# Second layer of three token blocks by seven half-size products instead of one full product

## The chip, the cores and the metric

The kernel runs on one core of one Trainium2 chip. The metric is the device time of one execution, in microseconds (us). The engines of the core are named as in the profile: PE (TensorE, matrix products), PEld (its weight loads), DVE (VectorE), ACT (ScalarE), POOL (GpSimd) and SP (SyncE, whose queue issues most transfers).

## The reference

Attention in two scales over 8 batches, 8 heads, 576 positions of 64 columns, then a two-layer network with ELU over all 4608 tokens:

```python
# attention, per head: a coarse one over means of 4 positions, repeated 4 times,
# and a local one over positions with |i - j| < 4
out_up = np.repeat(sm_attn(q_d, k_d, v_d), 4, axis=2)
x = (out_up + out_local)            # -> [4608 tokens, 512]
h = x @ w_in                        # [4608, 2048]
g = np.where(h > 0.0, h, np.exp(np.minimum(h, 0.0)) - 1.0)
return g @ w_out                    # [4608, 512] float32
```

## The kernel before, in words

The tokens are cut into nine blocks (0 to 8) of 512 tokens; a head batch `b` gives 576 tokens, so blocks and head batches overlap in time. Three kinds of work share the engines.

*Attention* (head batches 0 to 7): loads, casts from float32 to float16 on POOL (`cast_qk` L241, `cast_v` L302), transposes and scores on PE, exponentials on ACT, a mask on DVE (L496), denominators, outputs on PE into two-bank PSUM tiles, and `normalise` (L663): DVE multiplies by the reciprocals (L666, L671) and POOL adds local and coarse part into the block's input `xt` (L683).

*First layer*, `mm1(t, fc)` (L704): for block `t` and each of 16 groups `fc` of 128 hidden columns, four matmuls of 128x128 weights by 512 tokens (L719) fill a PSUM bank `hp` (two such banks, in turn). ELU follows in three operations: ACT takes the exponential (L723), DVE clamps it and subtracts one (L724), DVE takes max(h, 0) plus that (L725) into `gts[t][:, fc, :]`, in float16, hidden columns on the partitions.

*Second layer*, `mm2(t, i)` (L729): for each of four groups of 128 tokens, 16 matmuls (L739), four in each step `i`, take 128x128 of `gts[t]` as weights and 512 columns of `WO` (w_out) as the moving operand and add into a bank `op`; ACT copies it to `os` (L745) and SP sends it out (L747). The last token group of block 8 is done in two column parts, 384 and 128.

The order of everything is written by hand. Each piece of work is an event with a number, `at(number, function, ...)`; the events are sorted by number (L1014) and each engine runs its instructions in the order in which they were traced, so a waiting instruction holds all those behind it on its engine. The numbers are a plan, about one unit for each step of the first layer: `mm1_at(t, i)` is `51.52 + 16*(t-3) + i` for blocks from 4 on, and `mm2_at(t, i)` is `mm1_at(t+1, 0) + 0.5 + i`. So step `i` of the first layer of block `t+1` alternates on PE with step `i` of the second layer of block `t`. Below, "slot" is such a unit counted from the first layer step 0 of the block in hand. The second layer of block 8 has no first layer beside it and is the tail. The attention of a head batch is placed by a list of numbers (`LATER`, L977, for batches 4 to 6, `LAST`, L978, for batch 7), relative to the first layer of the block of the same number; `cast`, `tr`, `sc` and `out` are the casts, transposes, scores and outputs of its four head pairs.

Memory is taken from pools of tiles; a tile with the same tag and `bufs=n` takes turns in n places and waits until the place is free. PSUM has eight banks: two `misc`, two tiles of two banks for attention (`two`, L134), and from the end of batch 0 on two `hp` banks.

## Time and profile before

| | us |
|---|---|
| timed runs, median of three | 354.37 |
| timed runs, lowest and highest | 353.4 and 357.04 |
| profiled execution, span from the first to the last instruction | 353.6 |
| first layer of block 6 begins (PE, L719) | 249.15 |
| first layer of block 7 begins | 281.46 |
| last copy from PSUM begins (ACT, L745) | 350.81 |

The profile gives no time outside the span. In its rows "L739" is line 739 of the kernel, "out<-in" are the tiles written and read, and a busy time with "x4" is that of four instructions merged into one row. "idle before" is time in which the engine stood still ahead of the instruction, with the instruction that ended it behind the arrow. Matmuls overlap in the pipeline of PE, so a matmul's own duration is longer than its distance to the next; the distance is what counts.

### The profile page before, as it was taken

The numbers are of one execution on the slowest core, as the hardware profiler recorded it, in microseconds if no ns is written. First come the engines' busy times: TensorE is split into PE (matmuls) and PEld (weight loads), VectorE is DVE, ScalarE is ACT, GpSimd is POOL, SyncE is SP. The second block draws the span as 40 slices with busy tenths as digits, with TensorE's granted clock in tenths as the row PEclk, the third lists the DMA queues.
The fourth block names the chain that finished last, engine by engine and source line by source line (L and its number), as shares of the span: only waits on it lengthen the run. The fifth ranks groups of instructions, "written<-read, shape, count | busy, mean of one in ns | idle before, by whom it ended". The sixth has DMA issues, their size and how long they took to land.

```text
span 353.6 us, 10486 instructions
## 1 busy us (share of the span) xinstructions
PE 335.8 (95%) x4288; PEld 185.3 (52%) x4288; DVE 236.2 (67%) x466; ACT 180.6 (51%) x312; POOL 160.0 (45%) x298
## 2 busy tenths in 40 slices
PE   8897998899889998899999999999999999999996
PEld 4665784455455544445555555545455544444443
DVE  2316999665878775977797789779756955555510
ACT  3572795256665653466355636663553444444421
POOL 4563458286875841973396449755300600000000
PEclk9998999879989999999999999999999999999999
DMA  9999997899998869898979797953014010010012
GB/s 177 201 209 192 213 208 152 200 213 190 188 185 158 167 139 181 168 190 158 196 150 214 158 214 155 168 131 54 30 35 116 32 59 31 32 52 37 32 59 89
DMA packets 98768, 48.89 MB, mean 138 GB/s; under 512 B 81617, under 2 KB 93217, under 8 KB 98721
## 3 DMA queue, kind: packets, MB, share of 16 engines
q1 hardware_dynamic: 94417, 41.86, 58.7%
q0 software_dynamic: 4064, 6.26, 10.0%
q8 instruction: 33, 0.54, 0.7%
q10 hardware_dynamic: 240, 0.11, 0.2%
q14 instruction: 14, 0.11, 0.1%
HBM read 41.97 MB, written 9.55 MB: 146 GB/s over the span
## 4 chain that ended last, share of the span: by engine, by line
PE 75%; DVE 13%; DMA 6%; issue 3%; ACT 3%; SPq 0%; DVEq 0%; ACTq 0%
PE op L739 31%; PE hp L719 28%; DVE gt L725 4%; DMA rcb<-rd 3%; DVE e L724 3%; DVE ln L671 2%; DMA rd<-rc 2%; PE sc L758 2%; PE tqk L328 2%; PE sc L458 2%; PE lg L602 1%; ACT e L723 1%; PE vs L405 1%; PE lg L622 1%; PE den L518 1%
## 5 line engine op out<-in xcount | busy, mean ns | idle before, releaser
L739 PE MATMUL op<-WO,gt 128*128 128x512 f16 (+2 forms) x592 | 146.0, 375 | 0.5 <-DVE gt L725 0.5
L723 ACT ACTIVATE e<-hp 128x512 f16<-128x512 f32 x144 | 86.2, 599 | 107.1 <-PE hp L719 95.3
L719 PE MATMUL hp<-xt,WI 128*128 128x512 f16 x512 | 133.7, 385 | 1.4 <-DVE gt L725 1.3
L725 DVE SCALAR_TENSOR_TENSOR gt<-hp,e 128x512 f16<-128x512 f32 x144 | 99.6, 692 | 6.4
L724 DVE TENSOR_SCALAR e<-e 128x512 f16<-128x512 f16 x144 | 60.6, 421 | 58.4 <-ACT e L723 58.0
L739 PEld LDWEIGHTS <-gt 128*128 128x128 f16 x592 | 55.4, 98 | 61.7 <-issue 1.6
L719 PEld LDWEIGHTS <-WI 128*128 128x128 f16 x512 | 55.6, 115 | 50.0 <-issue 3.2
L683 POOL TENSOR_TENSOR xt<-ln 128x128 f16<-128x128 f16 (+7 forms) x55 | 36.6, 693 | 56.9 <-DVE ln L671 56.9
L481 ACT ACTIVATE pex<-sc 128x580 f16<-128x580 f32 (+1 forms) x56 | 30.1, 594 | 9.2 <-PE sc L471 8.6
L302 POOL CAST v<-v 128x640 f16<-128x640 f32 (+1 forms) x32 | 23.7, 741 | 20.4 <-DMA v<-in_v_dram 13.6
L394 POOL TENSOR_TENSOR t<-qt 128x288 f32<-128x288 f16 x27 | 18.1, 670 | 31.4 <-ACT qt L358 31.4
L745 ACT COPY os<-op 128x512 f32<-128x512 f32 (+2 forms) x37 | 21.4, 578 | 18.9 <-PE op L739 18.8
L377 DVE TENSOR_REDUCE ke<-kt 128x145 f16<-128x580 f16 x28 | 21.0, 751 | 2.4 <-ACT kt L365 2.4
L358 ACT COPY qt<-tqk 128x576 f16<-128x576 f16 x28 | 17.9, 639 | 8.4 <-PE tqk L328 7.7
L671 DVE TENSOR_TENSOR ln<-lg,rcb 128x580 f16<-128x580 f32 x28 | 21.1, 752 | 0.0
L241 POOL CAST k<-k 96x768 f16<-96x768 f32 x24 | 19.8, 825 | 0.1
L241 POOL CAST q<-q 96x768 f16<-96x768 f32 x24 | 19.6, 818 | 0.0
L698 PE MATMUL hp<-xt,WI 128*128 128x256 f16 x128 | 17.0, 283 | 0.7 <-DVE v L276 0.4
L496 DVE TENSOR_TENSOR pex<-pex,MASK 128x580 f16<-128x580 f16 x28 | 13.6, 486 | 3.0 <-ACT pex L481 2.8
L698 PEld LDWEIGHTS <-WI 128*128 128x128 f16 x128 | 13.3, 116 | 1.9 <-issue 0.8
L396 POOL TENSOR_TENSOR qd<-t 128x144 f16<-128x144 f32 x27 | 12.1, 448 | 2.1
L458 PEld LDWEIGHTS <-kt 64*64 64x64 f16 x560 | 6.9, 109 | 11.2 <-issue 8.6
(113 smaller groups left out, 273.4 us busy)
## 6 DMA issues: line engine op xcount, KB each, us to landing
out_dram<-os SPq DMA_DIRECT2D x35, 256.0 KB, 2.1
v<-in_v_dram SPq DMA_DIRECT2D x111, 80.0 KB, 4.5
q<-in_q_dram SPq DMA_DIRECT2D x25, 288.0 KB, 3.9
k<-in_k_dram SPq DMA_DIRECT2D x25, 288.0 KB, 5.0
rcb<-rd SPq DMA_DIRECT2D x10, 364.0 KB, 5.1
WI<-in_moe_w_in_dram POOLq DMA_DIRECT2D x4, 512.0 KB, 7.9
WO<-in_moe_w_out_dram POOLq DMA_DIRECT2D x4, 512.0 KB, 7.4
q<-in_q_dram POOLq DMA_DIRECT2D x7, 144.0 KB, 8.5
```

Of the source, the lines that this page charges most:

```text
L241: nc.gpsimd.tensor_copy(out=x[:], in_=src)
L302: nc.gpsimd.tensor_copy(out=v16[:], in_=v32[:].rearrange("p (e c) d -> p c e d", e=2))
L481: nc.scalar.activation(out=s["p"][:, :, a : a + n], in_=g2(sc, a, n), func=AF.Exp, scale=SCALE / 16 if a else SCALE,)
L671: nc.vector.tensor_tensor(out=ln[:, 0 : 2 * WL].rearrange("p (m h u) -> p m h u", h=2, u=WQ), in0=_free(lg[:, 0:1], [[WQ, WM], [512, 2], [ ...
L683: eng.tensor_tensor(out=xt(t)[:, j, t0 - TBLK * t : t1 - TBLK * t], in0=ln[:, a:z], in1=_rep4(ln[:, ga : ga + (z - a) // 4]), op=AB.add,)
L698: nc.tensor.matmul(FS[i][:, 256 * f : 256 * f + 256], w_in(dc, 2 * n + f), xts[0][:, dc, 256 * h : 256 * h + 256], start=(f == dc == 0), s ...
L719: nc.tensor.matmul(hp, w_in(dc, fc), xts[t][:, dc, :], start=(dc == 0), stop=(dc == DMC - 1),)
L723: nc.scalar.activation(out=e, in_=hp, func=AF.Exp)
L724: nc.vector.tensor_scalar(out=e, in0=e, scalar1=1.0, scalar2=-1.0, op0=AB.min, op1=AB.add)
L725: nc.vector.scalar_tensor_tensor(out=to, in0=hp, scalar=0.0, op0=AB.max, in1=e, op1=AB.add)
L739: nc.tensor.matmul(op_[:, a:z], gts[t][:, fc, 128 * tt : 128 * tt + 128], WO[:, fc, a:z], start=(fc == 0), stop=(fc == FCN - 1),)
L745: nc.scalar.copy(out=os_[:, a:z], in_=op_[:, a:z])
```

## The change

The second layer of blocks 6, 7 and 8 (`SW = 6`) is computed as a product of 2x2 halves. Tokens, hidden columns and output columns are halved (256, 1024, 256), and seven products of sums and differences of the halves (Winograd's form of Strassen's scheme) take the place of eight. A block has two units `u` of 128 rows of each token half. A product of a unit is eight matmuls of 128x128 weights by 256 columns: 112 matmuls of 256 columns a block instead of 64 of 512.

- `weights_7`: eight DVE subtractions of 128x1024 float16 make four difference matrices of `WO`, once. They stand from 0.6 to 14.6 units after the last cast of batch 7, that is from slot 11.75 of block 5's first layer to slot 9.75 of block 6's, two units apart.
- `sums_7`: for each group of four first-layer steps, four operations of 128x512 float16 make the sums of `gts[t]`; one of them overwrites a quarter of it. Groups 0 to 2 run on POOL, group 3 on DVE.
- the first layer of blocks 6 to 8 takes the hidden groups in the order 0, 8, 1, 9, ..., so that partners come together.
- `product` and `finish`: products 1, 6, 5, 3 add up in one half of a bank `y`, product 2 and products 7, 4 in the two halves of a bank `xz`; ACT copies the state after 1, 6 and 7 to SBUF; DVE adds in `finish` 4 (128x512) and `finish` 5 (128x256), ACT copies in `finish` 3. For blocks 6 and 7 the products of a unit stand at slots 0.5, 1.5, 2.5, 3.5, 4.5, 5.5 and 7.5 (plus 8 for the second unit), in the order 1, 2, 7, 6, 4, 5, 3; `finish` 4 and 5 stand 0.6 behind their product, `finish` 3 stands 0.1 behind. For block 8 both units are interleaved in the tail.
- `y` and a second tile `hx` take the four banks that attention used, once it is over; blocks 7 and 8 use `hx` as two further banks of the first layer.
- in blocks 7 and 8, for steps with `i % 8` in (1, 2, 5, 6, 7), ELU runs as Relu(-h) and Exp(-that) on ACT and one DVE operation, max(e - 1, h).
- tiles that are dead by then move to pools (`lo`, `tu`) which are closed, and the new tiles lie in their place.

The diff, cut to its core:

```diff
+SW = 6
+BELOW = (1, 2, 5, 6, 7)
...
-    def mm1(t, fc):
+    def mm1(t, i):
+        fc = i if t < SW else i // 2 + 8 * (i % 2)
...
-            hp, to = bank("hp", "hp")[:], gts[t][:, fc, :]
+            spare = late.get("x") if i % 4 > 1 else None
+            hp = spare[:, 512 * (i % 2) :][:, 0:512] if spare else bank("hp", "hp")[:]
+            to = gts[t][:, fc, :]
...
+        if t > SW and i % 8 in BELOW:
+            r = sb.tile([128, TBLK], FP32, tag="os", bufs=3, name="r")[:]
+            nc.scalar.activation(out=r, in_=hp, func=AF.Relu, scale=-1.0)
+            nc.scalar.activation(out=e, in_=r, func=AF.Exp, scale=-1.0)
+            nc.vector.scalar_tensor_tensor(
+                out=to, in0=e, scalar=-1.0, op0=AB.add, in1=hp, op1=AB.max
+            )
+            return
...
+    def weights_7(n, c):
+        T, k = W7["T"], slice(4 * c, 4 * c + 4)
+        b11, b12 = WO[:, k, 0:MH], WO[:, k, MH:DM]
+        b21, b22 = WO[:, FH + 4 * c :, 0:MH][:, 0:4], WO[:, FH + 4 * c :, MH:DM][:, 0:4]
+        x, y = ((b12, b11), (b22, T[:, 0, k]), (b22, b12), (b21, T[:, 1, k]))[n]
+        nc.vector.tensor_tensor(out=T[:, n, k], in0=x, in1=y, op=AB.subtract)
+
+    def sums_7(t, g):
...
+        S, G, k, l = S7[t], gts[t], slice(2 * g, 2 * g + 2), slice(FH + 2 * g, FH + 2 * g + 2)
+        a11, a12, a21, a22 = G[:, k, 0:TH], G[:, l, 0:TH], G[:, k, TH:TBLK], G[:, l, TH:TBLK]
+        eng = nc.vector if g == 3 else nc.gpsimd
+        for to, x, y, op in (
+            (S[:, 0, k], a21, a22, AB.add), (a21, a11, a21, AB.subtract),
+            (S[:, 1, k], S[:, 0, k], a11, AB.subtract), (S[:, 2, k], a12, S[:, 1, k], AB.subtract),
+        ):
+            eng.tensor_tensor(out=to, in0=x, in1=y, op=op)
+
+    def close_attention():
+        late["x"], late["y"] = two("hx"), two("y")
...
+    def product(t, u, n, k0=0, k1=FH):
+        xz, y, sn, ou = unit(t, u)
+        G, S, T = gts[t], S7.get(t), W7["T"]
+        a, b = slice(128 * u, 128 * u + 128), slice(TH + 128 * u, TH + 128 * u + 128)
+        to = y[:, 0:MH] if n in (1, 3, 5, 6) else xz[:, 0:MH] if n == 2 else xz[:, MH:DM]
+        for k in range(k0, k1):
+            w, x = (
+                (G[:, k, a], WO[:, k, 0:MH]), (G[:, FH + k, a], WO[:, FH + k, 0:MH]),
+                (S[:, 2, k, a], WO[:, FH + k, MH:DM]), (G[:, FH + k, b], T[:, 3, k]),
+                (S[:, 0, k, a], T[:, 0, k]), (S[:, 1, k, a], T[:, 1, k]), (G[:, k, b], T[:, 2, k]),
+            )[n - 1]
+            nc.tensor.matmul(
+                to, w, x, start=(k == 0 and n in (1, 2)), stop=(k == FH - 1),
+                skip_group_check=n > 2,
+            )
+        if k1 == FH and n in (1, 6, 7):
+            nc.scalar.copy(out=sn[:, {1: 0, 6: 1, 7: 2}[n], :], in_=to)
+
+    def finish(t, u, n):
...
+        if n == 4:
+            nc.vector.tensor_tensor(
+                out=ou[:, :, 0:MH], in0=xz[:].rearrange("p (c m) -> p c m", c=2), in1=sn[:, 0:2, :],
+                op=AB.add,
+            )
+        if n == 5:
+            nc.vector.tensor_tensor(out=ou[:, 1, MH:DM], in0=to, in1=sn[:, 2, :], op=AB.add)
+            nc.sync.dma_start(out=out[z : z + 128], in_=ou[:, 1, :])
+            if (t, u) == (NT - 1, 1):
+                nc.sync.dma_start(out=out[r : r + 128, 0:MH], in_=ou[:, 0, 0:MH])
+        if n == 3:
+            nc.scalar.copy(out=ou[:, 0, MH:DM], in_=to)
+            m0 = MH if (t, u) == (NT - 1, 1) else 0
+            nc.sync.dma_start(out=out[r : r + 128, m0:DM], in_=ou[:, 0, m0:DM])
...
-            if 16 * t + i <= 16 * NT - 4:
+            if t < SW:
                 at(mm2_at(t, i), mm2, t, i)
+    at(PLAN[B - 1]["cast"][3] + 0.05, close_feed)
+    at(PLAN[B - 1]["tr"][3] + 0.05, close_turn)
+    for n in range(4):
+        for c in range(2):
+            at(PLAN[B - 1]["cast"][3] + 0.6 + 2 * (2 * n + c), weights_7, n, c)
+    for t in range(SW, NT):
+        for g in range(4):
+            x = mm1_at(t, 4 * g + 3) + 0.05
+            if (t, g) == (SW, 2):
+                x = max(x, max(PLAN[B - 1]["out"]) + 0.1)
+            at(x, sums_7, t, g)
+        z = mm2_at(t, 0)
+        if t < NT - 1:
+            for u in range(2):
+                for n, x in zip((1, 2, 7, 6, 4, 5, 3), (0, 1, 2, 3, 4, 5, 7)):
+                    at(z + 8 * u + x, product, t, u, n)
+                    if n in (4, 5, 3):
+                        at(z + 8 * u + x + (0.1 if n == 3 else 0.6), finish, t, u, n)
+        else:
+            steps = [(u, n, 0, FH - 1) for u in range(2) for n in (1, 2)]
+            steps += [(u, n, FH - 1, FH) for u in range(2) for n in (1, 2)]
+            steps += [(u, n) for u, n in ((0, 7), (0, 6), (1, 7), (1, 6), (0, 4), (0, 5), (1, 4), (1, 5), (0, 3), (1, 3))]
+            for n, x in enumerate(steps):
+                at(z + n, product, t, *x)
+                if x[1] in (4, 5, 3):
+                    at(z + n + 0.1, finish, t, *x)
+    at(mm1_at(SW + 1, 0) - 0.1, close_attention)
```

More of the change, by code (lines that the diff above doesn't have):

```diff
@@ L120, in const @@
     def const(a, name, queue):
-        t = C[name] = sb.tile(list(a.shape), FP16, tag=name, bufs=1, name=name)
+        pool = sb if name in ("ID", "MASK", "IND2", "VR2") else lo
+        t = C[name] = pool.tile(list(a.shape), FP16, tag=name, bufs=1, name=name)
         queue.dma_start(out=t[:], in_=nc.inline_tensor(a, name=name + "c").ap())
+    feed = ctx.enter_context(ExitStack())
+    turn = ctx.enter_context(ExitStack())
+    lo = feed.enter_context(tc.tile_pool(name="lo", bufs=1, side="right"))
+    tu = turn.enter_context(tc.tile_pool(name="tu", bufs=1))
     front = ctx.enter_context(ExitStack())
@@ L175, in load_wo @@
         nc.gpsimd.dma_start(out=WO[:, 4 * n : 4 * n + 4, :], in_=src)
-    KD = [sb.tile([128, 2 * KG + 16], FP16, tag=f"kd{i}", bufs=1, name="kd") for i in range(4)]
+    KD = [lo.tile([128, 2 * KG + 16], FP16, tag=f"kd{i}", bufs=1, name="kd") for i in range(4)]
     KE = [sb.tile([128, 192], FP16, tag=f"ke{i}", bufs=1, name="ke") for i in range(4)]
@@ L391, in sums @@
         else:
-            t2 = sb.tile([128, 2 * SD], FP32, tag="pex", bufs=2, name="t2")
+            t2 = tu.tile([128, 2 * SD], FP32, tag="pex", bufs=2, name="t2")
             at_ = src.rearrange("p (g f) -> p f g", f=2)
@@ L730, in mm2 @@
         tt, part = i // 4, i % 4
-        cols = ((0, DM),)
-        if t == NT - 1 and tt == 3:
-            cols, part = ((0, 384), (384, DM)), 0
-        for a, z in cols:
-            if part == 0:
-                ops[(t, tt)] = bank("misc", "op")
-            op_ = ops[(t, tt)]
-            for fc in range(4 * part, 4 * part + 4 if len(cols) == 1 else FCN):
-                nc.tensor.matmul(
-                    op_[:, a:z], gts[t][:, fc, 128 * tt : 128 * tt + 128], WO[:, fc, a:z],
-                    start=(fc == 0), stop=(fc == FCN - 1),
-                )
-            if part == 3 or len(cols) == 2:
-                os_ = sb.tile([128, DM], FP32, tag="os", bufs=3, name="os")
-                nc.scalar.copy(out=os_[:, a:z], in_=op_[:, a:z])
-                r = TBLK * t + 128 * tt
-                nc.sync.dma_start(out=out[r : r + 128, a:z], in_=os_[:, a:z])
+        if part == 0:
+            ops[(t, tt)] = bank("misc", "op")
@@ new lines, in mm2 @@
+        op_ = ops[(t, tt)]
+        for fc in range(4 * part, 4 * part + 4):
+            nc.tensor.matmul(
+                op_[:], gts[t][:, fc, 128 * tt : 128 * tt + 128], WO[:, fc, :],
+                start=(fc == 0), stop=(fc == FCN - 1),
+            )
+        if part == 3:
+            os_ = sb.tile([128, DM], FP32, tag="os", bufs=3, name="os")
+            nc.scalar.copy(out=os_[:], in_=op_[:])
+            r = TBLK * t + 128 * tt
+            nc.sync.dma_start(out=out[r : r + 128], in_=os_[:])
@@ new lines, with close_feed, close_turn @@
+    W7, S7, U7 = {}, {}, {}
+    MH, TH, FH = DM // 2, TBLK // 2, FCN // 2
+    def close_feed():
+        feed.close()
+        late["w"] = ctx.enter_context(tc.tile_pool(name="w7", bufs=1, side="right"))
+        W7["T"] = late["w"].tile([128, 4, FH, MH], FP16, tag="T", name="w7")
+    def close_turn():
+        turn.close()
+        late["s"] = ctx.enter_context(tc.tile_pool(name="s7", bufs=1))
+    def weights_7(n, c):
[4 more added lines that the diff above has]
+        nc.vector.tensor_tensor(out=T[:, n, k], in0=x, in1=y, op=AB.subtract)
@@ new lines, in sums_7 @@
+    def sums_7(t, g):
+        if g == 0:
+            S7[t] = late["s"].tile([128, 3, FH, TH], FP16, tag="S", bufs=2, name="s7")
+        S, G, k, l = S7[t], gts[t], slice(2 * g, 2 * g + 2), slice(FH + 2 * g, FH + 2 * g + 2)
[6 more added lines that the diff above has]
+            eng.tensor_tensor(out=to, in0=x, in1=y, op=op)
@@ new lines, in close_attention, with unit @@
+    def close_attention():
+        late["x"], late["y"] = two("hx"), two("y")
+    def unit(t, u):
+        if (t, u) not in U7:
+            z, y = bank("misc", "xz"), late["y"][:, 512 * u :][:, 0:512]
+            sn = late["s"].tile([128, 3, MH], FP32, tag="sn", bufs=2, name="sn")
+            ou = late["s"].tile([128, 2, DM], FP32, tag="ou", bufs=2, name="ou")
+            U7[(t, u)] = z, y, sn, ou
+        return U7[(t, u)]
+    def product(t, u, n, k0=0, k1=FH):
[9 more added lines that the diff above has]
+            )[n - 1]
+            nc.tensor.matmul(
+                to, w, x, start=(k == 0 and n in (1, 2)), stop=(k == FH - 1),
[3 more added lines that the diff above has]
+            nc.scalar.copy(out=sn[:, {1: 0, 6: 1, 7: 2}[n], :], in_=to)
@@ L750 @@
     act, dve = nc.scalar.copy, nc.vector.tensor_copy
-    Z = sb.tile([128, 512], FP16, tag="Z", bufs=1, name="Z")
+    Z = lo.tile([128, 512], FP16, tag="Z", bufs=1, name="Z")
     def keep(t, n):
@@ L826, in selections @@
         else:
-            src = sb.tile([KW, 16], FP16, tag="I4", bufs=1, name="I4")
+            src = lo.tile([KW, 16], FP16, tag="I4", bufs=1, name="I4")
             nc.vector.tensor_reduce(
```

24 lines of the change are left out of this document (14 added, 10 removed).

## The prediction

> **What bounds the kernel now.** I read the busy shares first, then the chain that ended last, then a table of busy time over the stretches of the last blocks.
>
> ```profile
> span 353.6 us, 10486 instructions
> PE 335.8 (95%) x4288; PEld 185.3 (52%) x4288; DVE 236.2 (67%) x466; ACT 180.6 (51%) x312; POOL 160.0 (45%) x298
> ...
> PE 75%; DVE 13%; DMA 6%; issue 3%; ACT 3%; SPq 0%; DVEq 0%; ACTq 0%
> ```
> ```profile
> 213.00:247.40 34.40, 34.35 (x472) 17.92 (x471) 28.32 (x51) 19.59 (x35) 24.28 (x47) 1.00 0.68 130
> 247.40:280.70 33.30, 33.27 (x395) 17.14 (x395) 23.77 (x47) 15.48 (x27) 7.11 (x13) 1.00 0.19 56
> 280.70:308.40 27.70, 27.70 (x130) 13.49 (x128) 16.36 (x33) 11.91 (x20) 0.96 (x1) 1.00 0.10 39
> 308.40:336.00 27.60, 27.60 (x129) 13.46 (x128) 15.78 (x32) 11.91 (x20) 0.00 (x0) 1.00 0.10 39
> 336.00:354.00 18.00, 14.73 (x85) 7.45 (x82) 0.99 (x2) 3.69 (x7) 0.00 (x0) 1.00 0.19 73
> ```
> In the second fence the columns behind the stretch are its length and the busy time of PE, PEld, DVE, ACT and POOL, then the granted clock. In the first layer of blocks 6, 7 and 8 (stretches two, three and four) and in the tail TensorE never waits, at full clock. Any time it is given less work is won, and any wait that it gets is lost, one for one. DVE is the next engine: 28.3 of 34.4 us in the stretch with the outputs of head batch 6, 16 of 28 later.
>
> **Part 1, fewer columns through TensorE: minus 4.4 us.** One regular slot, and the only products of 256 columns with a full 128x128 weight tile, at full clock:
>
> ```profile
> 331.54 1.03 PE L719 MATMUL hp<-xt,WI 128*128 128x512 f16 x4
> 331.83 0.69 DVE L725 SCALAR_TENSOR_TENSOR gt<-hp,e 128x512 f16<-128x512 f32 x1
> ...
> 332.40 1.03 PE L739 MATMUL op<-WO,gt 128*128 128x512 f16 x4
> 332.60 0.60 ACT L723 ACTIVATE e<-hp 128x512 f16<-128x512 f32 x1 [1.13 <-PE hp L719]
> ...
> 333.23 0.29 DVE L724 TENSOR_SCALAR e<-e 128x512 f16<-128x512 f16 x1 [0.70 <-ACT e L723]
> 333.26 1.03 PE L719 MATMUL hp<-xt,WI 128*128 128x512 f16 x4
> 333.56 0.69 DVE L725 SCALAR_TENSOR_TENSOR gt<-hp,e 128x512 f16<-128x512 f32 x1
> ```
> ```profile
> 37.21 3.68 PE L698 MATMUL hp<-xt,WI 128*128 128x256 f16 x32 [0.31 <-DVE gt L725]
> 41.28 1.03 PE L698 MATMUL hp<-xt,WI 128*128 128x256 f16 x8 [0.39 <-DVE v L276]
> ```
> ```profile
> L698 PEld LDWEIGHTS <-WI 128*128 128x128 f16 x128 | 13.3, 116 | 1.9 <-issue 0.8
> ```
> From 331.54 to 333.26 are eight matmuls of 512 columns: 1.72 us, 0.216 each (the last one's shown end includes its drain). Of 256 columns, 24 more take 3.68 - 1.03 = 2.65 us, 0.110 each, so weight loads don't bind. A block's second layer goes from 64 x 0.216 = 13.8 us to 112 x 0.110 = 12.4: 1.45 saved, 4.4 in three blocks. Bounds: 5.2 if 256 columns cost just half (0.108), 2.5 if each costs the 0.116 that its weight load shows.
>
> **Part 2, a new wait in each unit: plus 6.8 us.** A unit's y bank takes product 1, then 6, 5 and 3 on top; between 5 and 3 DVE must have read it (finish 5). By the order of events, product 5 stands at slot 5.5, finish 5 at 5.5 + 0.6 = 6.1, the first layer's step 6 at 6.0, product 3 at 7.5. So finish 5 is queued on DVE behind the ELU of step 6, whose matmul runs only after product 5; and step 6 is one of those (i mod 8 in 1, 2, 5, 6, 7) with two ACT passes. Product 3 waits for all of it, with everything behind it on PE's queue.
>
> ```profile
> L745 ACT COPY os<-op 128x512 f32<-128x512 f32 x35 | 20.6, 590 | 16.5 <-PE op L739 16.4
> L671 DVE TENSOR_TENSOR ln<-lg,rcb 128x580 f16<-128x580 f32 x28 | 21.1, 752 | 0.0
> L666 DVE TENSOR_TENSOR ln<-lg,rcb 128x144 f16<-128x144 f32 x28 | 8.4, 300 | 6.2 <-DMA rcb<-rd 3.9 <-PE lg L622 2.2
> L791 ACT CAST vd<-vs 96x256 f16<-96x256 f32 x4 | 1.5, 364 | 0.0
> L238 ACT ACT_TABLE_LOAD x1 | 1.3, 1283 | 1.6 <-PEq L1030 1.6
> ```
> ```profile
> 250.22 0.60 ACT L723 ACTIVATE e<-hp 128x512 f16<-128x512 f32 x1 [0.23 <-PE hp L719]
> 250.71 1.07 ACT L481 ACTIVATE pex<-sc 128x580 f16<-128x580 f32 x2
> ```
> ```profile
> 242.06 0.75 DVE L671 TENSOR_TENSOR ln<-lg,rcb 128x580 f16<-128x580 f32 x1
> 242.73 0.76 DVE L724 TENSOR_SCALAR e<-e 128x512 f16<-128x512 f16 x1
> ```
> From the end of step 6 on PE (the slot above: 332.40): ACT starts after 0.20; Relu 0.60 (as the copy of that shape, L745); Exp, now from SBUF, 0.63 (the trace has none of this shape; from below 0.5, if it begins in its forerunner's last 0.1 as the ACT rows at 250 do, from above 0.7); 0.03 to DVE; the last ELU operation 0.69; finish 5, 128x256 from PSUM, 0.42 (0.300 + 112 x 452/436 ns, between L666 and L671), beginning 0.08 before its forerunner's end as the second of the two DVE rows does; about 0.08 to PE. Sum 2.57. PE has step 7 to do meanwhile, 0.86. Wait 1.7 us a unit, four units (two each for blocks 6 and 7, in the steps of blocks 7 and 8): 6.8 us. Bounds: 4 x 1.4 = 5.6 and 4 x 2.2 = 8.8 (another ACT or DVE instruction of 0.5 in front). What product 3 holds up is all later PE work, so nothing gives it back. The other edges are covered: product 6 needs ACT's copy of product 1, three slots (5 us) earlier, 0.36 (L791); finish 4 (0.69) frees no bank of this unit.
>
> The Trainium skill, "ScalarE: Activation LUTs", section "Rules for kernel authors", says to do relu on VectorE and not ScalarE, which speaks against moving the clamp. By the profile's rows VectorE takes 0.29 where Relu takes about 0.60; by that rule the chain would be 0.3 us shorter and the four waits 5.4 us, so the rule alone would not save the change.
> A table load at each change between Relu and Exp would be 40 x 1.28 = 51 us; with copies and Exps mixed all along, ACT has loaded once (L238), and I count none.
>
> Four PSUM banks give the ELU steps four slots instead of two before PE needs the bank again; they remove waits of which the trace has none here (stretches three and four), so I count nothing. ACT gains 20 passes of 0.6, 6 us in each of two stretches of 27.6 with 11.9 busy: no bound.
>
> **Part 3, weight differences on DVE: plus 1.2 us.** Eight operations of 128x1024. L496 (580 columns, both inputs f16 in SBUF) and its range give 0.15 + 1024 x 0.52 ns = 0.68 each:
>
> ```profile
> L496 DVE TENSOR_TENSOR pex<-pex,MASK x28: 450/461/829, 45.2 to 259.8; 128x580 f16<-128x580 f16 x28
> ```
> ```profile
> 246.68 0.69 DVE L725 SCALAR_TENSOR_TENSOR gt<-hp,e 128x512 f16<-128x512 f32 x1
> ```
> ```profile
> 246.34 1.03 PE L739 MATMUL op<-WO,gt 128*128 128x512 f16 x4
> 247.43 1.02 PE L719 MATMUL hp<-xt,WI 128*128 128x512 f16 x4
> ```
> The first stands (11.75 in block 5's slots) between the outputs of head batch 6 (11.71) and step 12: in the middle of DVE's stretch without a pause, from 242.73. Step 13's ELU ends at 247.37 there, and PE starts step 15, which needs its bank, at 247.43. Pushed by 0.68 it makes PE wait about 0.6. The second stands behind step 13's ELU and pushes again; DVE has made good only part: another 0.6. The other six find 0.70 of DVE idle per slot, as in Part 1's slot, and cost nothing; without that cover, 0.6 each. Bounds: 0 and 2.2 (each held by GpSimd up to 829 - 450 ns, L496's range).
>
> **Part 4, sums on GpSimd: plus 0.2 us.** Twelve operations a block:
>
> ```profile
> L683 POOL TENSOR_TENSOR xt<-ln 128x512 f16<-128x512 f16 x4 | 4.3, 1070 | 0.0
> ```
> ```profile
> L724 DVE TENSOR_SCALAR e<-e x144: 278/295/1036, 36.1 to 336.7; 128x512 f16<-128x512 f16 x144
> ```
> ```profile
> 279.00 2.66 POOL L683 TENSOR_TENSOR xt<-ln 128x64 f16<-128x64 f16 x4 [1.84 <-DVE ln L671]
> ```
> ```profile
> 281.46 1.03 PE L719 MATMUL hp<-xt,WI 128*128 128x512 f16 x4
> ```
> 4 x 1.07 = 4.3 us a group, 13 of 26 us a block, on an engine that is idle there. Block 6's third group begins after 281.66; product 7 reaches its part of it at about 286.2 (step 0 of block 7 at 281.46, five groups of 0.87 later, four matmuls in) and needs two of the four operations: 283.8. Beside GpSimd, DVE's clamp lasts up to 1.04 instead of 0.29; PE's slack on the bank is 333.26 - 332.52 = 0.7, so only holds near 1 us show, in block 6 alone (two banks): 0.2, bounds 0 and 1.
>
> **Part 5, the tail: plus 0.4 us.** Its saving is in Part 1. In its order each wait is covered (product 6 comes two other products after product 1's end, 0.6 us behind ACT's copy; the last product 3 comes one product after product 5's end, 0.2 us behind finish 5), so PE runs through; at the end
>
> ```profile
> 350.81 0.27 ACT L745 COPY os<-op 128x128 f32<-128x128 f32 x1 [0.41 <-PE op L739]
> ```
> the last copy has 256 columns instead of 128, 0.36 against 0.27, and its 128 KB queue behind 640 KB of the last two microseconds, where now 64 follow 192. Bounds 0.1 and 1.5.
>
> **Sum.** -4.4 + 6.8 + 1.2 + 0.2 + 0.4 = +4.2, on a span of 353.6. The profile gives nothing outside the span; the three runs' median, 354.37, is 0.8 above it. So 354.4 + 4.2 = 358.6 us.
>
> **Rivals.** (a) The waits of Part 2 don't arise: DVE reads y before step 6's ELU, or ACT's two passes pipeline away, so that finish 5 is done within PE's 0.86 us. For it: in the whole trace PE waits for DVE at L739 only 0.5 us. Against: DVE's rows follow the written order everywhere, and the distance is three times the cover. It turns the verdict when a wait falls under 0.6 us. Time 354.4 - 4.4 + 1.8 = 351.8; (b) with DVE's pushes of Part 3 hidden too, 350.4, faster. (c) The waits come at half their size, one ACT pass hidden: 355.2. (d) Weight loads bind the 256-column products: 1.9 less saved, 360.5; the 0.110 above speaks against it. (e) GpSimd's sums, slowed by DVE's two-input operations, come late for product 7 and DVE's own sums, 1 to 2 us in block 6: about 360.2.
>
> **How the numbers follow.** Forecast 0.47, (a) 0.12, (b) 0.18, (c) 0.13, (d) 0.03, (e) 0.07. A measurement tells about 1%, 3.5 us. Faster by more than that: (b) and a little of (a), 0.22. Within: the rest of (a), (c) and the forecast's lower part, 0.33. Slower: 0.45. The forecast's own range, from the bounds, is 356.3 to 361.0; to hold 8 in 10 it must reach to (a) and most of (b): 350.4 to 360.6.
>
> **What would show it.** Right: in the rows of the changed kernel, product 3 waits for DVE's add some 1.7 us, four times; 112 matmuls a block at 0.110; PE waits of half a microsecond near 247 to 250; the chain goes through ACT and DVE at step 6. Wrong: no PE wait for DVE over 0.6 us in blocks 7 and 8, DVE's add ahead of step 6's ELU, or many waits elsewhere (product 7 on GpSimd, table loads on ACT).

## The result, and the profile after

The changed kernel takes 374.65 us (median of 4 runs, 372.23 to 376.63), the kernel before on the same chip 353.97 (median of 4). The ratio is 1.0587, 95% interval 1.0517 to 1.0658: 20.7 us slower, where 4.2 slower were forecast. The profiled execution of the changed kernel took 373.94 us with a span of 372.2, so 1.7 us lie outside the span, where the forecast put 0.8.

First lines and the chain that ended last, of the changed kernel's page:

```profile
span 372.2 us, 10833 instructions
PE 334.7 (90%) x4416; PEld 197.8 (53%) x4416; DVE 256.1 (69%) x478; ACT 194.3 (52%) x343; POOL 203.9 (55%) x334
...
PE 64%; DMA 13%; DVE 12%; ACT 4%; issue 2%; POOL 2%; SPq 1%; DVEq 0%; POOLq 0%; ACTq 0%
```

TensorE is busy for 334.7 us instead of 335.8, in a span that is 18.6 longer: the time is in waits of TensorE, and PE's share of the chain falls from 75 to 64%. The stretches of the last blocks, cut near the same steps as in the kernel before (start and end; length, then busy time of PE, PEld, DVE, ACT and POOL, the granted clock, the share of the DMA engines, GB/s):

```profile
213.00:249.90 36.90, 36.00 (x480) 18.70 (x478) 30.84 (x53) 20.20 (x36) 26.42 (x49) 1.00 0.73 122
249.90:283.20 33.30, 32.78 (x392) 16.52 (x391) 31.78 (x54) 15.63 (x27) 17.13 (x19) 1.00 0.20 56
283.20:319.70 36.50, 28.59 (x178) 18.86 (x178) 20.60 (x31) 18.46 (x34) 19.07 (x17) 0.95 0.08 29
319.70:355.00 35.30, 28.31 (x178) 18.64 (x177) 18.64 (x32) 19.15 (x36) 13.73 (x12) 0.95 0.08 31
355.00:372.30 17.30, 12.74 (x112) 10.72 (x110) 3.60 (x8) 2.98 (x8) 0.00 (x0) 0.98 0.21 76
```

The stretches with the first layers of blocks 7 and 8 (third and fourth row) lasted 27.7 and 27.6 us before, without a pause on PE; now 36.5 and 35.3, with PE idle for 7.9 and 7.0 and a clock of 0.95. What PE waits for from 230 us on (engine, its instruction, who ended the wait: us in total, times, longest):

```profile
PE hx L729 <- DVE gt L737: 14.4, 8, 2.6
PE hp L729 <- DVE gt L743: 1.4, 2, 0.9
PE y L821 <- ACT ou L844: 0.9, 2, 0.5
PE y L821 <- DVE ou L839: 0.5, 1, 0.5
PE y L821 <- ACT sn L826: 0.4, 1, 0.4
```

14.4 of 17.6 us are a wait that the prediction does not have: a first-layer step in the tile `hx` waits for VectorE's last ELU operation. The eight are one of 2.57, four of 2.07 and three of 1.20. The forecast wait, product 3 for finish 5, does not come in the first layers of blocks 7 and 8 (the row of 0.5 is in the tail). One of the eight, in the changed kernel's timeline of all engines (start, us, engine, instruction, in brackets the wait ahead of it):

```profile
295.51 1.04 PE L821 MATMUL y<-w,s 128*128 128x256 f16 x8
...
296.38 1.03 PE L729 MATMUL hx<-xt,WI 128*128 128x512 f16 x4
...
297.44 0.60 ACT L735 ACTIVATE r<-hx 128x512 f32<-128x512 f32 x1 [0.47 <-PE hx L729]
...
298.07 0.63 ACT L736 ACTIVATE e<-r 128x512 f16<-128x512 f32 x1
298.74 0.69 DVE L737 SCALAR_TENSOR_TENSOR gt<-e,hx 128x512 f16<-128x512 f16 x1 [0.44 <-ACT e L736]
299.34 0.42 DVE L839 TENSOR_TENSOR ou<-y,sn 128x256 f32<-128x256 f32 x1
299.48 1.32 PE L729 MATMUL hx<-xt,WI 128*128 128x512 f16 x4 [2.07 <-DVE gt L737]
```

The step at 296.38 is step 6, in the first bank of `hx`; step 7 is to fill the second bank, which is free, and yet starts only at 299.48, when step 6 has gone through Relu, Exp and the last ELU operation. Finish 5 (299.34, 0.42 long) runs in that wait too, and is over by the time that product 3 asks for it. The two banks of `hx` are one tile of 1024 columns, and the program orders the tile, not its banks: its matmuls wait for every read of it.

The size of the wait follows from what stands around it: 2.07 where step `i + 1` comes straight behind step `i`, 1.20 where a product of 0.87 us lies between them. The one of 2.57 is step 3 of block 7. There the ELU itself came late, behind the four sums of block 6's last group on VectorE (`sums_7`, 284.50 to 288.93), which the forecast did not price:

```profile
284.50 0.53 DVE L796 TENSOR_TENSOR s<-gt 128x512 f16<-128x512 f16 x1
285.07 1.26 DVE L796 TENSOR_TENSOR gt<-gt 128x512 f16<-128x512 f16 x1
286.25 1.38 DVE L796 TENSOR_TENSOR s<-s,gt 128x512 f16<-128x512 f16 x1
287.67 1.26 DVE L796 TENSOR_TENSOR s<-gt,s 128x512 f16<-128x512 f16 x1
```

### The profile page after: what moved, and what is told of

Read it like the earlier page. It is cut to its first block, busy times and chain, and to the rows that moved or that the text cites. A ratio compares the mean times of both kernels' runs of the same rounds, so it can differ in the third digit from the quotient of the medians.

```text
span 372.2 us, 10833 instructions
## 1 busy us (share of the span) xinstructions
PE 334.7 (90%) x4416; PEld 197.8 (53%) x4416; DVE 256.1 (69%) x478; ACT 194.3 (52%) x343; POOL 203.9 (55%) x334
## 4 chain that ended last, share of the span: by engine, by line
PE 64%; DMA 13%; DVE 12%; ACT 4%; issue 2%; POOL 2%; SPq 1%; DVEq 0%; POOLq 0%; ACTq 0%
PE hp L729 21%; PE op L753 17%; PE y L821 6%; DMA v<-in_v_dram 6%; DMA rcb<-rd 5%; PE hx L729 4%; DMA rd<-rc 3%; PE xz L821 3%; DVE ln L678 2%; PE sc L857 2%; DVE gt L743 2%; DVE e L742 2%; DVE gt L737 2%; PE sc L465 1%; PE tqk L335 1%
## 5 line engine op out<-in xcount | busy, mean ns | idle before, releaser
L729 PE MATMUL hp<-xt,WI 128*128 128x512 f16 x448 | 118.6, 388 | 3.3 <-DVE gt L743 2.7
L741 ACT ACTIVATE e<-hp 128x512 f16<-128x512 f32 x120 | 71.8, 599 | 86.0 <-PE hp L729 78.9
L753 PE MATMUL op<-WO,gt 128*128 128x512 f16 x384 | 98.6, 380 | 0.0
L742 DVE TENSOR_SCALAR e<-e 128x512 f16<-128x512 f16 x124 | 62.1, 501 | 40.4 <-ACT e L741 39.7
L729 PEld LDWEIGHTS <-WI 128*128 128x128 f16 x512 | 55.5, 115 | 62.7 <-issue 21.4
L743 DVE SCALAR_TENSOR_TENSOR gt<-hp,e 128x512 f16<-128x512 f32 x120 | 83.0, 692 | 5.6
L401 POOL TENSOR_TENSOR t<-qt 128x288 f32<-128x288 f16 x27 | 18.6, 689 | 31.2 <-ACT qt L365 31.2
L796 POOL TENSOR_TENSOR s<-gt 128x512 f16<-128x512 f16 x9 | 11.1, 1228 | 38.6 <-PE hp L729 19.5
L729 PE MATMUL hx<-xt,WI 128*128 128x512 f16 x64 | 17.3, 395 | 14.4 <-DVE gt L737 14.4
L821 PEld LDWEIGHTS <-s 128*128 128x128 f16 x144 | 14.9, 104 | 6.4 <-issue 2.2
L737 DVE SCALAR_TENSOR_TENSOR gt<-e,hx 128x512 f16<-128x512 f16 x12 | 8.3, 688 | 14.1 <-ACT e L736 14.1
```

What stands on the lines that cost most here:

```text
L729: nc.tensor.matmul(hp, w_in(dc, fc), xts[t][:, dc, :], start=(dc == 0), stop=(dc == DMC - 1),)
L741: nc.scalar.activation(out=e, in_=hp, func=AF.Exp)
L742: nc.vector.tensor_scalar(out=e, in0=e, scalar1=1.0, scalar2=-1.0, op0=AB.min, op1=AB.add)
L743: nc.vector.scalar_tensor_tensor(out=to, in0=hp, scalar=0.0, op0=AB.max, in1=e, op1=AB.add)
L753: nc.tensor.matmul(op_[:], gts[t][:, fc, 128 * tt : 128 * tt + 128], WO[:, fc, :], start=(fc == 0), stop=(fc == FCN - 1),)
L821: nc.tensor.matmul(to, w, x, start=(k == 0 and n in (1, 2)), stop=(k == FH - 1), skip_group_check=n > 2,)
```

## The experiments

The first three runs follow the waits, the next four VectorE and the weight differences, four more the buffers and the loads, and the last one the weight differences again. Ratios are against the kernel before on the same chip, with 95% intervals. "From block 7 on" is the time from the start of block 7's first layer to the end of the span: 281.46 to 353.6 = 72.1 us before, 283.23 to 372.2 = 89.0 in the changed kernel.

### e1_own_tiles: each bank a tile of its own

```diff
-            hp = spare[:, 512 * (i % 2) :][:, 0:512] if spare else bank("hp", "hp")[:]
+            hp = spare[i % 2][:] if spare else bank("hp", "hp")[:]
...
-        late["x"], late["y"] = two("hx"), two("y")
+        attn.close()
+        four = ctx.enter_context(
+            tc.tile_pool(name="four", bufs=1, space=bass.MemoryType.PSUM, side="right")
+        )
+        late["x"], late["y"] = (
+            [four.tile([128, 512], FP32, tag=f"{n}{i}", bufs=1, name=n) for i in range(2)]
+            for n in ("hx", "y")
+        )
...
-            z, y = bank("misc", "xz"), late["y"][:, 512 * u :][:, 0:512]
+            z, y = bank("misc", "xz"), late["y"][u]
```

(The attention's two-bank tiles move to a pool of their own, `attn`, so that their banks can be given to the four tiles.)

> The four late PSUM banks as four tiles of one bank each (hx0, hx1, y0, y1) instead of two tiles of two banks; nothing else changed. Theory (one tile, one order): in the changed kernel each first-layer step i with i % 4 = 3 waits for the ELU of step i - 1 because both write one tile hx, although into different banks; so here the eight waits of PE for DVE at hx (14.4 us) vanish, the granted clock stays at 1.00 in blocks 7 and 8, and the wait that was forecast takes their place: product 3 waits for finish 5 some 1.2 to 1.8 us, four times. Time 357 to 361, near 359. Rival (ELU too slow): two ACT passes a step make the ELU chain longer than the banks allow, whatever tile they lie in; then PE keeps waiting 10 us or more at the same steps and the time stays above 368.

357.61 us, ratio 1.0178 (1.0112 to 1.0244), against 1.0587: 0.041, or 14.5 us, come back. From block 7 on 281.11 to 355.5 = 74.4. What PE waits for from 230 us on, and the timeline where the waits on `hx` were:

```profile
PE y L830 <- DVE ou L848: 6.2, 4, 1.5
PE hp L731 <- DVE gt L745: 1.4, 2, 0.9
```
```profile
291.53 1.89 PE L731 MATMUL hx<-xt,WI 128*128 128x512 f16 x8
...
292.59 0.60 ACT L737 ACTIVATE r<-hx 128x512 f32<-128x512 f32 x1 [0.48 <-PE hx L731]
...
293.22 0.63 ACT L738 ACTIVATE e<-r 128x512 f16<-128x512 f32 x1
...
293.88 0.69 DVE L739 SCALAR_TENSOR_TENSOR gt<-e,hx 128x512 f16<-128x512 f16 x1 [0.45 <-ACT e L738]
...
294.49 0.42 DVE L848 TENSOR_TENSOR ou<-y,sn 128x256 f32<-128x256 f32 x1
294.96 1.03 PE L830 MATMUL y<-WO,s 128*128 128x256 f16 x8 [1.54 <-DVE ou L848]
```

The stretch of block 7's first layer in e1, with the clock at 1.00:

```profile
281.11:310.55 29.44, 26.36 (x178) 18.14 (x178) 20.69 (x33) 18.49 (x34) 19.01 (x17) 1.00 0.08 28
```

Steps 6 and 7 now run in one go (eight matmuls from 291.53), and behind them stands the wait that the prediction named: product 3 for finish 5, four times. That the tile is what serialised the steps is shown.

### e2_finish5_first: finish 5 ahead of the ELU of step 6

```diff
-                        at(z + 8 * u + x + (0.1 if n == 3 else 0.6), finish, t, u, n)
+                        at(z + 8 * u + x + {3: 0.1, 4: 1.2, 5: 0.1}[n], finish, t, u, n)
```

(On top of e1; finish 4 comes after finish 5, and the row's transfer moves behind finish 4.)

> As the run with four tiles, and finish 5 placed 0.1 behind its product (ahead of step 6's ELU on DVE), finish 4 with the row's transfer behind it, in blocks 6 and 7. Theory (order on DVE): product 3's wait falls from 1.2 to 1.8 us to under 0.4, so 4 to 6 us less than the run with four tiles: 352 to 355. Rival (the wait is for DVE's load, not its order): product 3 still waits over 1 us, and the time is within 1.5 us of the run with four tiles.

351.98 us, ratio 1.0016 (0.9976 to 1.0057). The wait on finish 5 is gone. What PE waits for from 230 us on, and the stretch of block 7's first layer:

```profile
PE hp L731 <- DVE gt L745: 1.4, 2, 0.9
```
```profile
285.27:311.31 26.04, 26.04 (x177) 18.17 (x177) 19.96 (x31) 17.49 (x33) 19.01 (x17) 1.00 0.09 31
```

PE runs through, at full clock, in 26.04 us; the same stretch took 29.44 in e1, 36.26 in the changed kernel (283.23 to 319.49) and 27.6 before. From block 7 on it is 285.27 to 352.9 = 67.6 us, 4.5 less than before; so it is in every run built on this one (67.6 to 67.7). And still the total is no better than before. By the ratio it is 0.6 us above it, so some 5 us are lost ahead of block 7.

How much of that lies where can't be read from this trace alone: its execution took 354.66 us, the longest of the ten. The part ahead of block 5 differs by several microseconds between traces of the same instructions: block 5's first layer begins at 215.57 us in the kernel before and at 209.27 in e9 below, whose computation is the same. The granted clock differs there too: 0.89 from 30 to 45 us and 0.77 from 60 to 75 in the one, 1.00 in both stretches of the other. So terms of a few microseconds ahead of block 5 are taken from the ratios of the runs below.

### e3_two_banks: the changed kernel without `hx`

```diff
-            spare = late.get("x") if i % 4 > 1 else None
+            spare = None
```

> The changed kernel with the first layer of blocks 7 and 8 in its two hp banks only (hx is allocated and not used). Theory (one tile): waits at hx are gone with the tile; with two banks a step waits for the ELU two steps back, whose chain of about 2.2 us has 2.6 us, so waits of 0 to 0.5 us, and product 3's wait for finish 5 of 1.2 to 1.8 us, four times, appears: 358 to 364, more than 10 us under the changed kernel though it has fewer banks. Rival (ELU too slow): fewer banks make it worse, at or above 374.

363.11 us, ratio 1.0325 (1.0251 to 1.0398): the two banks more, as the change uses them, make it slower than none, by 0.026 of the time, 9 us. What PE waits for from 230 us on, the first three rows:

```profile
PE y L821 <- DVE ou L839: 4.7, 5, 1.1
PE hp L729 <- DVE gt L743: 4.5, 3, 3.1
PE hp L729 <- DVE gt L737: 1.3, 4, 0.3
```

The total is in the range expected and the rival is wrong: the longer ELU chain alone costs four waits of 0.33 (third row), and product 3's wait for finish 5 is there four times, 1.05 each (first row). Not expected was the wait of 3.10 (second row): step 2 of block 7 needs the bank of step 0, whose ELU stands behind the four sums of block 6 on VectorE. With four tiles (e1) none of the waits of the second and third row comes in blocks 7 and 8. So two banks more are worth something there once they are tiles of their own: e1 lies 0.015 of the time, 5.2 us, under this run, give or take 3.5.

### e4_weights_later: the weight differences in block 6's stage

```diff
-            at(PLAN[B - 1]["cast"][3] + 0.6 + 2 * (2 * n + c), weights_7, n, c)
+            at(mm1_at(SW, 0) + 1.6 + 1.5 * (2 * n + c), weights_7, n, c)
```

(On top of e2.)

> As the run with finish 5 first, and the eight weight differences from step 1.6 to step 12.1 of block 6's first layer, after the outputs of head batch 6, instead of from step 11.75 of block 5's. Theory (DVE had no pause there): the two waits of PE for DVE just ahead of block 6 (0.87 and 0.52 us in the changed kernel) vanish: 1 to 2 us less than the run with finish 5 first, so 350.5 to 353. Rival (they only move): the same time, with the waits in block 6.

351.83 us, ratio 1.0003 (0.9968 to 1.0038), as e2. The first layer of block 5 took 33.58 us before, 35.10 in e2 and 33.57 here; that of block 6 took 32.31, 32.41 and 34.55. The cost moves with the operations, from one stage to the next, and does not shrink (PE waits 1.9 us for VectorE at `hp` here, 1.4 in e2): the rival was right.

### e6_elu_block6 and e7_small_pieces: VectorE in block 6, smaller pieces

```diff
-        if t > SW and i % 8 in BELOW:
+        if t >= SW and i % 8 in BELOW:
```
```diff
-        T, k = W7["T"], slice(4 * c, 4 * c + 4)
+        T, k = W7["T"], slice(2 * c, 2 * c + 2)
...
-        for c in range(2):
-            at(PLAN[B - 1]["cast"][3] + 0.6 + 2 * (2 * n + c), weights_7, n, c)
+        for c in range(4):
+            at(mm1_at(SW, 0) + 0.6 + 0.65 * (4 * n + c), weights_7, n, c)
```

(Each on top of e2.)

> The kernel with four single-bank tiles and finish 5 ahead of the ELU, with one edit: the ELU whose minus 1 and clamp lie on ScalarE is used in block 6's ten steps as well. It takes ten clamps off VectorE in the stage in which VectorE is busiest (31.6 of 33.1 us in the changed kernel). Theory (VectorE bounds block 6's stage): up to 10 x 0.3 = 3 us less in that stage, a total of 349 to 351. Rival (TensorE bounds it, and VectorE is only full because its waits fit): no change within 1 us; and since block 6 has one bank pair for its first layer, a chain that is longer by one ScalarE operation may add a wait on ScalarE of some tenths a step, up to 2 us more.

> The kernel with four single-bank tiles and finish 5 ahead of the ELU, with one edit: the weight differences in sixteen pieces of 128x512 instead of eight of 128x1024, one every 0.65 us of the plan from the first step of block 6 on. In block 5's stage the eight pieces cost 1.5 us, moved whole into block 6's stage 2.2. Theory (a piece of 0.7 to 1.1 us delays the ELU behind it by about its own length, and half a piece fits the slack of a step): block 6's stage 0.5 to 1 us above its 32.4, block 5's back at 33.6, a total of 0.5 to 1.5 us less than with finish 5 first alone. Rival (what counts is VectorE's sum of work in a full stage, not the size of one piece): block 6's stage 2 us longer again, the total the same within 0.7 us.

352.74 us, ratio 1.0012 (0.9972 to 1.0052), and 352.81, ratio 1.0033 (1.0006 to 1.0060): neither can be told from e2. VectorE is full in block 6's stage (31.78 of 33.30 us in the changed kernel), yet with ten clamps less there the stage does not get shorter (32.74 us in e6, 32.41 in e2). In e7 it takes 35.36, in e4 with eight pieces 34.55; sixteen pieces leave 2.5 us of waits of PE on VectorE, eight 1.9. Both rivals were right.

### e8_no_weights: no weight differences

```diff
-                (S[:, 2, k, a], WO[:, FH + k, MH:DM]), (G[:, FH + k, b], T[:, 3, k]),
-                (S[:, 0, k, a], T[:, 0, k]), (S[:, 1, k, a], T[:, 1, k]), (G[:, k, b], T[:, 2, k]),
+                (S[:, 2, k, a], WO[:, FH + k, MH:DM]), (G[:, FH + k, b], WO[:, k, 0:MH]),
+                (S[:, 0, k, a], WO[:, k, MH:DM]), (S[:, 1, k, a], WO[:, FH + k, 0:MH]), (G[:, k, b], WO[:, k, 0:MH]),
...
-    for n in range(4):
-        for c in range(2):
-            at(PLAN[B - 1]["cast"][3] + 0.6 + 2 * (2 * n + c), weights_7, n, c)
```

> The kernel with four single-bank tiles and finish 5 ahead of the ELU, without the weight differences: the four products that need them multiply by plain quarters of the weights instead, so the output is not the reference's in blocks 6 to 8. Theory (they cost the 1.5 us by which block 5's stage grew): a total 1.2 to 2.2 us below the one with finish 5 first, block 5's stage at 33.6 and block 6's at 32.4. Rival (the stage grew for another reason, as the sums on GpSimd or where transfers land): block 5's stage stays at 35, the total within 0.7 us.

350.35 us, ratio 0.9957 (0.9921 to 0.9992), 0.006 or 2.1 us under e2, give or take 1.9. In the traces block 5's first layer is back at 33.57 us and block 6's is 32.62, together 1.3 us less than in e2; PE waits for `hp` no more. The rest of the 2.1 is within the two intervals.

### e5_pools_only: the kernel before, with the buffers where the change puts them

```diff
-        t = C[name] = sb.tile(list(a.shape), FP16, tag=name, bufs=1, name=name)
+        pool = sb if name in ("ID", "MASK", "IND2", "VR2") else lo
+        t = C[name] = pool.tile(list(a.shape), FP16, tag=name, bufs=1, name=name)
...
-            t = sb.tile([QB, 2 * NB, D], FP32, tag=name + "32", bufs=3, name=name + "32")
+            t = lo.tile([QB, 2 * NB, D], FP32, tag=name + "32", bufs=3, name=name + "32")
...
+    at(PLAN[B - 1]["cast"][3] + 0.05, feed.close)
+    at(PLAN[B - 1]["tr"][3] + 0.05, turn.close)
```

(And so for all tiles that the change moves to `lo` and `tu`.)

> The kernel before with one thing of the change alone: the buffers of the attention that die early stand in pools of their own, closed at the same two steps of the plan; the computation is that of the kernel before. Finish 5 ahead of the ELU gave a kernel that saves 4.5 us from block 7 on, pays 1.5 for the weight differences in block 5's stage, and yet measured 0.0 against before where about 3 less was due. Theory (the placement or its closing costs time in the first half): 2 to 3 us more than before, a ratio of 1.006 to 1.009, block 7's and block 8's stages as before. Rival (the placement is free, the first half only varies from run to run): a ratio of 1.000, within 0.003.

354.09 us, ratio 1.0083 (1.0046 to 1.0120): 2.9 us, with the same instructions in the same order. It is the row of the hardware queue in the list of transfers that differs (packets, megabytes, and the time of the packets as a share of sixteen engines' span). Of the kernel before, with the three kinds of load whose targets moved (count, KB each, median us from issue to landing):

```profile
q1 hardware_dynamic: 94417, 41.86, 58.7%
...
v<-in_v_dram SPq DMA_DIRECT2D x111, 80.0 KB, 4.5
q<-in_q_dram SPq DMA_DIRECT2D x25, 288.0 KB, 3.9
k<-in_k_dram SPq DMA_DIRECT2D x25, 288.0 KB, 5.0
```

The same of e5:

```profile
q1 hardware_dynamic: 94417, 41.86, 65.5%
...
v<-in_v_dram SPq DMA_DIRECT2D x111, 80.0 KB, 5.4
q<-in_q_dram SPq DMA_DIRECT2D x25, 288.0 KB, 4.8
k<-in_k_dram SPq DMA_DIRECT2D x25, 288.0 KB, 6.2
```

And the same row of the changed kernel, then of e2:

```profile
q1 hardware_dynamic: 94417, 41.86, 61.2%
```
```profile
q1 hardware_dynamic: 94417, 41.86, 63.5%
```

The same packets and the same bytes keep the engines busy for 65.5 instead of 58.7% of nearly the same span. As shares of their spans that is 208 us before, 232 in e5, and 228 and 224 in the changed kernel and in e2. The targets lie elsewhere, and by the layout of the buffers their addresses start otherwise: beyond a multiple of 256 bytes by 128 (q32, k32) and 160 (v32) in the kernel before, by 224 for all three in e5.

### e9, e10, e11: the start addresses

Unused bytes ahead of the buffers set the start. Of e9 (e5 with the starts of before), of e10 (the kernel before with all starts at multiples of 256) and of e11 (e2, all starts at multiples of 256):

```diff
+    sb.tile([128, 224], FP16, tag="pad", bufs=1, name="pad")
     Z = lo.tile([128, 512], FP16, tag="Z", bufs=1, name="Z")
+    lo.tile([128, 112], FP16, tag="pad1", bufs=1, name="pad1")
...
+            lo.tile([128, 176], FP16, tag="pad2", bufs=1, name="pad2")
             t = C[name] = lo.tile([KW, 1280], FP16, tag=name, bufs=1, name=name)
```
```diff
+    sb.tile([128, 48], FP16, tag="pad1", bufs=1, name="pad1")
     V00 = sb.tile([KW, 2 * NB, D], FP32, tag="v32", bufs=3, name="v32")
...
     Z = sb.tile([128, 512], FP16, tag="Z", bufs=1, name="Z")
+    sb.tile([128, 16], FP16, tag="pad2", bufs=1, name="pad2")
```
```diff
+    sb.tile([128, 32], FP16, tag="pad", bufs=1, name="pad")
     Z = lo.tile([128, 512], FP16, tag="Z", bufs=1, name="Z")
...
+            lo.tile([128, 112], FP16, tag="pad2", bufs=1, name="pad2")
             t = C[name] = lo.tile([KW, 1280], FP16, tag=name, bufs=1, name=name)
```

> The kernel before with the pool moves alone and unused bytes ahead of the buffers, so that the targets of the loads (v32, q32, k32, q16, k16) have the same start address modulo 512 bytes as in the kernel before (160, 384, 384, 384, 384), though they lie elsewhere; with the moves alone they start at 224, 224, 224, 448, 448, the same bytes took 65.5 against 58.7% of the sixteen DMA engines, and the time was 1.0083 of before. Theory (the start address within 256 bytes sets how long a transfer's packets take): share back at 58 to 60%, ratio 1.000 within 0.004. Rival (the place in the memory or the closing of the pools costs the time): share 64 to 66%, ratio 1.006 to 1.010 again.

> The kernel before with nothing else but unused bytes ahead of two buffers, so that v32, q32, k32, q16 and k16 all start at a multiple of 256 bytes (before: 160 and 128 beyond one). Theory (the further the start lies beyond a multiple of 256, the longer the packets): from 128 and 160 to 224 the DMA share rose by 6.8 points and the time by 2.6 us; to 0 it falls by 6 to 12 points, to 47 to 53%, and the time by 2 to 4 us, 347.5 to 349.5. Rival (128 is as good as 0, the loss comes from 224 alone): share 58 to 59%, time as before within 1 us.

> The changed kernel with four single-bank tiles, finish 5 ahead of the ELU, and the targets of the loads at multiples of 256 bytes. Theory (the changed products' gain of 4.5 us was eaten by the start addresses, 2.6, and the weight differences, 1.5): the DMA share at 50 to 54%, a total 4 to 6 us below the 352.0 of the same kernel at 224, 346 to 348, 1 to 2 us below the kernel before with aligned targets. Rival (addresses count for nothing in this kernel): share 63%, 352 within 1 us.

The row of the hardware queue in e9, then in e10, then in e11:

```profile
q1 hardware_dynamic: 94417, 41.86, 60.0%
```
```profile
q1 hardware_dynamic: 94417, 41.86, 52.3%
```
```profile
q1 hardware_dynamic: 94417, 41.86, 52.4%
```

e9 takes 351.55 us, ratio 1.0004 (0.9965 to 1.0043): with the old starts in the new places the loss is gone, so it was the starts and neither the places nor the closing. (The unused bytes shift other buffers of the same pools too; that among them the targets of the loads are what counts is argued from the packets' time.) e10 takes 349.84, ratio 0.9978 (0.9941 to 1.0015): the share falls as expected, from 58.7 to 52.3%, but the time by 0.8 us at most likely and not by 2 to 4, which a measurement does not tell from none. There the theory holds for the packets and fails for the time. e11 takes 347.39, ratio 0.9914 (0.9888 to 0.9940), 0.010 or 3.6 us under e2 and 3.0 us under the kernel before: the lowest median so far, though within 1% of before. Its 347.39 lies in the range expected; the gain on e2 is a little less than the 4 to 6 us expected, the distance to e10 (349.84 on the same chip) a little more than the 1 to 2. The two pairs agree: 224 to 0 gives 3.6 us in e11, 128 and 160 to 0 gives 0.8 in e10, and their difference is near the 2.9 of e5.

The Trainium skill, "DMA: Bandwidth & Descriptors", section "How a descriptor splits into AXI transactions", says that a transaction starts at a multiple of 256 bytes, so that a run that begins beyond one pays for bytes that are not used. By its count of 32-byte beats, a run of 256 bytes (one position of one head, 64 float32) costs 8 beats at 0, 12 at 128, 13 at 160 and 15 at 224 (estimates from that page). The trace agrees in the order: 52.3, 58.7 and 60.0, and 65.5%. The page states it for reads, and here the start of the side that is written was moved.

### e12_half_weights_gpsimd: half of the weight differences on GpSimd

```diff
-        nc.vector.tensor_tensor(out=T[:, n, k], in0=x, in1=y, op=AB.subtract)
+        eng = nc.gpsimd if c else nc.vector
+        eng.tensor_tensor(out=T[:, n, k], in0=x, in1=y, op=AB.subtract)
...
-            at(PLAN[B - 1]["cast"][3] + 0.6 + 2 * (2 * n + c), weights_7, n, c)
+            x = (5.0, 5.1, 13.0, 15.5)[n] if c else 0.6 + 4 * n
+            at(PLAN[B - 1]["cast"][3] + x, weights_7, n, c)
```

(On top of e11.)

> The aligned kernel with finish 5 ahead of the ELU, with one edit: four of the eight weight differences on GpSimd, two between the attention's last sums and block 6's first ones and two behind block 6's second ones, where GpSimd was idle for 5.6 and 2.8 us and more; the four on VectorE one every 4 us of the plan. Without any weight differences the time was 2 us lower. Theory (what they cost is VectorE's sum of work): half of the 2 us comes back, 345.5 to 347 against the 347.4 of before this edit. Rival (GpSimd beside VectorE makes VectorE's own two-input operations longer, 0.68 to 1.1 us in the changed kernel, and four pieces of 2.4 us delay the sums and the normalised block behind them): nothing comes back or it costs up to 2 us, 347.5 to 349.5.

348.89 us, ratio 0.9902 (0.9868 to 0.9937): not to be told from e11's 0.9914, and in the range of the rival. The instructions on the tile of the differences in e12 (least, median and greatest ns, first and last start):

```profile
L786 DVE TENSOR_TENSOR w<-WO x2: 682/916/1151, 234.8 to 252.2; 128x1024 f16<-128x1024 f16 x2
L786 POOL TENSOR_TENSOR w<-WO x2: 2125/2151/2177, 241.8 to 266.1; 128x1024 f16<-128x1024 f16 x2
L786 POOL TENSOR_TENSOR w<-WO,w x2: 2125/2150/2176, 244.0 to 268.2; 128x1024 f16<-128x1024 f16 x2
L786 DVE TENSOR_TENSOR w<-WO,w x2: 681/1320/1960, 244.7 to 260.8; 128x1024 f16<-128x1024 f16 x2
```

The one piece on VectorE that meets a piece on GpSimd takes 1.96 us, and a clamp (L744, at 242.15) takes 1.95 instead of 0.28 beside the piece that GpSimd begins at 241.83. So VectorE gets little of the relief; PE's waits on VectorE for `hp` rise from 1.4 to 3.0 us.

## Why the prediction was wrong

The failing step is a sentence of Part 2: "Four PSUM banks give the ELU steps four slots instead of two before PE needs the bank again; they remove waits of which the trace has none here (stretches three and four), so I count nothing." It priced the banks and not the tile that holds them, and it set down as nothing a term that came to 14.6 us net. The two halves of `hx` are ordered as one tile, so step 7 needs not a bank of four steps ago but the end of its neighbour's whole chain: eight waits of 1.20 to 2.57 us. That both halves come from one tile stands in the diff (`spare[:, 512 * (i % 2) :]`); the question that Part 2 asked of `y` alone, which reads must be over before this matmul may write, would have led to it. The other half of the sentence fails too: e3, with two banks, has waits of 3.10 and four times 0.33 that four tiles remove. They come from what the change adds on VectorE and ScalarE, so the trace before could not show them. For `y` the same form costs 0.9 + 0.5 + 0.4 us in the tail.

With that undone, the other steps can be held against runs, mostly from block 7 on:

| step | forecast | measured |
|---|---|---|
| Part 1, fewer columns | -1.45 a block, -4.4 | 26.04 against 27.6 a block; 67.6 against 72.1 us from block 7 on, -4.5 |
| Part 2, product 3 waits for finish 5 | +6.8, four times 1.7 | e1 against e2: 74.4 - 67.6 = +6.8, four times |
| Part 2, two banks more | 0 | changed kernel against e1: 89.0 - 74.4 = +14.6 |
| Part 3, weight differences | +1.2, two waits of 0.6 | two waits, 0.9 and 0.5; +1.5 in block 5's first layer; e8 against e2 0.006 of the time, +2.1 |
| Parts 4 and 5, sums and tail | +0.2 and +0.4 | no wait of PE on GpSimd from 230 us on; from block 7 on -4.5 with the tail in it, where Part 1 alone is -4.4: about nothing. VectorE's own four sums, not priced: a wait of 3.10 in block 7 with two banks (e3), none with four tiles |
| start addresses of the loads | not considered | e5 against before, 0.0083: +2.9 |

Part 2's chain was right to 0.03 us in each term: 0.20, 0.60, 0.63, 0.03, 0.69 less the overlap, 0.42 (a gap of 0.03 between Relu and Exp was left out, and the step to PE is 0.05 and not 0.08). In e1 step 6 ends on PE at 292.39 (291.53 and four times 0.216) and product 3 starts at 294.96, 2.57 later, as forecast. The forecast of these parts was right and the verdict of the whole wrong in size, because a larger wait stood in front and hid this one: while step 7 waits for step 6's chain, finish 5 gets done.

e1 is the kernel that the prediction had in mind. By its ratio it is 6.3 us slower than before, give or take 2.3, against the 4.2 forecast; 2.9 of that are the start addresses. That its 357.61 us comes so near to the 358.6 forecast is in part luck, since the kernel before took 351.62 on that chip and not 354.4. The bounds of the parts, each at its worst, add up to 365.4, so no term of the sum within its bounds could have given 374.65. (How the narrower 356.3 to 361.0 follows from those bounds is not shown. In the sentence on Relu, 4 times 1.4 is 5.6 and not 5.4; nothing hangs on it.)

Where the 14.6 us are: 14.4 in the waits on `hx`; 1.4 in the eight ends of the pipeline ahead of them, which the profile counts as busy (0.17 each, a group's 1.03 less the 0.86 after which the next can start); 1.8 in the waits on `y`; 3.4 by the clock, which is below; and 6.8 less, since the wait for finish 5 lies inside them. That makes 14.2 of 14.6.

Rival (a), VectorE reading y before step 6's ELU, is what e2 builds, and there the four waits do not arise. No rival had `hx`, nor the last row of the table. The instructions of the attention are the same, so the prediction let the change begin at block 5; but it moves the targets of the loads, and e5 and e9 show that the kernel feels how long their packets take. Which steps of the attention the longer packets hold up was not followed, so that link is argued from the ratios and the packets' time.

By the ratios, times 354 us: tiles 14.5 (changed kernel against e1), order of finish 5 5.7 (e1 against e2), differences 2.1 (e2 against e8), start addresses 2.9 (e5), 25.2 in all; from the 20.7 measured that leaves -4.5 for the products themselves, beside Part 1's -4.4. Each of these terms has an interval of 1.3 to 3.4 us to either side, so the agreement to a tenth is chance. That the tile stands first is not; among the other three the intervals leave the order open.

## What to carry to other kernels

Before pricing a bank, ask what the program orders: two halves of one tile wait for each other as if they were one, and a buffer meant to give distance can take it away. A wait can hide another one of nearly its size, so that undoing the one that the trace shows may bring out the next. A change that moves buffers changes the start addresses of transfer targets: look at the packets' share of the DMA engines with the same bytes. Here 224 bytes beyond a multiple of 256 cost 2.9 us against 128 and 160; from there to 0 the packets got shorter again and the time did not measurably.
